# A gated-attention and mixing kernel: three stores behind a branch, and two chunks' z in one buffer

## The chip, the cores and the metric

The kernel runs on one core of a Trainium2 chip. The metric is device time in microseconds (us), the median of several executions of the same program. PE is the matrix engine, DVE the vector engine, ACT the scalar engine, POOL the general-purpose engine, and SP the engine that only issues transfers here. Each engine has its own instruction stream, executes it in order, and waits on semaphores that others count up.

## The reference

B=4, H=8, S=768, D=48. First a gated linear attention, then a token mixing of its output x (768 x 384 per batch) and a channel mixing:

```python
for t in range(S):
    state = f[:, :, t, :, None] * state + np.einsum('bhd,bhe->bhde', k[:, :, t], v[:, :, t])
    y[:, :, t] = np.einsum('bhd,bhde->bhe', q[:, :, t], state)
...
theta = x @ w_theta
zr, zi = x * np.cos(theta), x * np.sin(theta)
y = np.einsum('ts,bsd->btd', w_tok_r, zr) + np.einsum('ts,bsd->btd', w_tok_i, zi)
u = x + y
return u + np.maximum(u @ w_ch, 0.0)
```

## The kernel before

The sequence is cut into chunks of 128 tokens, six per batch, 24 in all. For every chunk the attention is computed in steps: gates (`gc`, `go`, `gs`, `ge`, `gq`, `gk`), scores, state, output (`ou`), copies of the output (`xc`, `xs`), then angles (`th`), their folding (`tn`, `se`, `ab`), sine and cosine (`tr`) and z = (x cos, x sin) (`ro`, line 434). The token mixing works on groups: two groups of 384 output tokens per batch, eight in all, and three slices of 128 channels in each; step `f` multiplies one chunk's z into one slice (L457, `pm`). After its last `f` a slice is added to x (`v`, L461), split in two float32r parts (`uh` on ACT, `ul` on DVE), run through the channel mixing (`c`, L475), finished with the maximum (`cv`, L489, DVE) and stored (`so`, L493, an SP transfer of 192 KB).

The weights are 64-bit words in memory. Sixteen parts of them are loaded (`lw`, tile `raw`, L171) and decoded in four steps: `d1` on DVE (L184), `d2` on ACT (L189), `d3` on DVE (L194, L195). Parts 2 to 13 are the token weights, 14 and 15 the channel weights `w_ch`. The raw parts and the z share one pool tag, `z`, of six buffers that are handed out in turn: the seventh tile asked for takes the buffer of the first, and its first writer waits until that one's last reader is done. In the first batch z is half as large as such a buffer, and each of its six chunks takes one.

The order on PE, ACT, DVE and POOL is written out by hand in the string table `ORDER`. SP is placed by the scheduler and executes its transfers in the order that it was given; a transfer that waits for a buffer holds up all behind it.

At the end stands a general path for inputs whose gates decay too far: a flag, computed by step `fl`, is read into a register on every engine (L575, TENSOR_LOAD), and each engine branches on it (L618). With these inputs the flag is zero and the path is skipped. On the skipping side every engine executes one EVENT_SEMAPHORE (SP eight, one for each semaphore of its transfers): it waits until all that the engine has issued is done and steps the count up by what the general path would have added, so that later waits are the same on both ways. A jump follows to the block behind the path (L690), in which SP waits for the transfers' semaphores and all engines meet twice before the program ends.

Of the kernel before, what the change touches and what calls it, by code (L numbers as in the profile page):

```python
# [8 lines left out]
F32 = mybir.dt.float32  # L9
# [8 lines left out]
B, H, S, D = 4, 8, 768, 48  # L18
DM = H * D
P = 128  # L20
NP = H // 2
C = 128
NC = S // C
HC = NC // 2
KD = DM // P
TH = 384
NTH = S // TH
# [56 lines left out]
)  # L84


# [1 line left out]
def gla_moe_kernel(  # L88
# [13 lines left out]
    nc = tc.nc  # L102

    const = ctx.enter_context(tc.tile_pool(name="const", bufs=1))
    sb = ctx.enter_context(tc.tile_pool(name="sb", bufs=1))
# [173 lines left out]
    def bank(shape, name):  # L279
        return ps.tile(shape, F32, tag="a", bufs=4, name=name)  # L280
# [95 lines left out]
    uts, xhs, xls, pths, ws, zs = ({} for _ in range(6))  # L376

    def u_tile(g):
        return sb.tile([P, KD, TH], F32, tag="ut", bufs=3, name=f"ut{g}")

    def u_slice(m):
        return uts[m // 3][:, :, m % 3 * C:(m % 3 + 1) * C]
# [6 lines left out]
    def split_xh(m, src):  # L389
        xhs[m] = sb.tile([P, KD, P], F32R, tag="xh", bufs=1, name=f"xh{m}")  # L390
        copy(nc.scalar, xhs[m], src)

    def split_xl(m, src):
        xls[m] = sb.tile([P, KD, P], F32R, tag="xl", bufs=1, name=f"xl{m}")
        nc.vector.tensor_tensor(xls[m], src, xhs[m], op=ALU.subtract)


    def angles(m, full):
        pths[m] = bank([P, DM], f"pth{m}")
        ms = ([(u_slice(m)[:, d, :], values[d // 2][:, d % 2, :]) for d in range(KD)] if full else  # L400
              [(l[:, d, :], r[:, d, :]) for l, r in ((xhs[m], wth[1]), (xhs[m], wth[0]), (xls[m], wth[1]))
               for d in range(KD)])
        for n, (l, r) in enumerate(ms):
            nc.tensor.matmul(pths[m], l, r, start=(n == 0), stop=(n == len(ms) - 1))  # L404
# [25 lines left out]
    def rotate(m, full):  # L430
        w = ws[m]
        if full:
            zs[m] = sb.tile([P, 2, DM], F32, tag="z", bufs=6, name=f"z{m}")
        nc.vector.tensor_tensor(zs[m] if full else w, w, xs[m].unsqueeze(1).to_broadcast([P, 2, DM]), op=ALU.mult)  # L434

    def split_zh(m):
        zs[m] = sb.tile([P, 2, 2, DM], F32R, tag="z", bufs=6, name=f"z{m}")
        copy(nc.scalar, zs[m][:, 1], ws[m])

    def split_zl(m):  # L440
        nc.vector.tensor_tensor(zs[m][:, 0], ws[m], zs[m][:, 1], op=ALU.subtract)
# [4 lines left out]
    def products(g, s, d, z, full):  # L446
        n, dsl = NTOK + g % NTH * NC + s, slice(d * P, (d + 1) * P)
        if s == 0:
            pms[g, d] = ps.tile([P, TH], F32, tag="mix", bufs=4, name=f"pm{g}{d}")

        if full:
            ms = [(z[:, i, dsl], values[n][:, 1 - i, :]) for i in range(2)]
        else:
            w = parts[n][2]
            ms = [(z[:, a, i, dsl], w[o][:, 1 - i, :]) for i in range(2) for a, o in ((1, 1), (1, 0), (0, 1))]
        for i, (l, r) in enumerate(ms):
            nc.tensor.matmul(pms[g, d], l, r, start=(s == 0 and i == 0), stop=(s == NC - 1 and i == len(ms) - 1))  # L457
# [33 lines left out]
    def store(b, g, d):  # L491
        th = g % NTH
        nc.sync.dma_start(out[b, d * P:(d + 1) * P, th * TH:(th + 1) * TH], uts[g][:, d, :])  # L493


    flag = const.tile([P, 1], I32, tag="flag", name="flag")
# [45 lines left out]
    def group(fn):  # L542
        return lambda n: fn(n // KD, n % KD)
# [5 lines left out]
    fn = {"h" + s: lambda n, go=go: go(n // 2, n % 2) for s, go in by_halves.items()}  # L549
# [12 lines left out]
        "f": piece, "v": group(add_u), "uh": group(split_uh), "ul": group(split_ul), "c": channels, "cv": group(finish),  # L562
        "so": group(lambda g, d: store(g // NTH, g, d)), "fl": find_worst,
    }
    done, engines = {}, {"": None, "A": nc.scalar, "D": nc.vector, "P": nc.gpsimd}
    for step in " ".join(ORDER).split():
        step, _, e = step.partition("/")
        m = done[step] = done.get(step, -1) + 1
# [3 lines left out]
    order.__exit__(None, None, None)  # L572


    rv = nc.values_load(flag[0:1, 0:1], min_val=0, max_val=P)  # L575

    def recurrence(b):
        pick = sb.tile([P, 2 * P], F32, tag="p", bufs=1, name="pick")
        nc.vector.memset(pick, 0.0)
        nc.vector.memset(pick[0:32, 47:48], 1.0)  # L580
        nc.vector.memset(pick[32:48, 47:48], 1.0)
        nc.vector.memset(pick[64:96, 111:112], 1.0)
        nc.vector.memset(pick[96:112, 111:112], 1.0)
        for p in range(NP):
            ld = []
            for nm, src in (("f", f), ("k", k), ("q", q)):
                t = sb.tile([P, NC, C], F32, tag="ut", bufs=3, name=f"r{nm}{p}")
                nc.sync.dma_start(t, src[b, :, :, p, :].rearrange("c r t -> r c t"))
                ld.append(t.rearrange("r c t -> r (c t)"))
            fr, kr, qr = ld  # L590
            zr = [sb.tile([P, 2, S], F32, tag="z", bufs=6, name=f"rz{p}{n}") for n in range(3)]
            vr, st, yt = zr[0][:, 0, :], zr[1][:, 0, :], zr[2][:, 0, :]
            kvs = [zr[0][:, 1, :], zr[1][:, 1, :]]
            nc.sync.dma_start(vr, vt[b, p])
            nc.scalar.activation(fr, fr, AF.Sigmoid)
            acc = [ps.tile([P, TH], F32, tag="mix", bufs=4, name=f"acc{p}{h}") for h in range(NTH)]
            for e in range(D):

                sel = sb.tile([P, 2, 64], F32, tag="w", bufs=2, name=f"sel{p}{e}")
                for j in range(2):  # L600
                    nc.vector.tensor_copy(sel[:, j, :], ident[:, 64 * j + e:64 * j + e + 1].to_broadcast([P, 64]))
                kv = kvs[e % 2]
                for h in range(NTH):
                    hs = slice(h * TH, (h + 1) * TH)
                    bc = bank([P, TH], f"bc{p}{e}{h}")
                    nc.tensor.matmul(bc, sel.rearrange("p j m -> p (j m)"), vr[:, hs], start=True, stop=True)
                    nc.vector.tensor_tensor(kv[:, hs], kr[:, hs], bc, op=ALU.mult)
                nc.vector.tensor_tensor_scan(st, fr, kv, 0.0, ALU.mult, ALU.add)
                nc.vector.tensor_tensor(kv, qr, st, op=ALU.mult)
                for h in range(NTH):  # L610
                    nc.tensor.matmul(acc[h], pick[:, 47 - e:47 - e + P], kv[:, h * TH:(h + 1) * TH],
                                     start=(e == 0), stop=(e == D - 1))
            for h in range(NTH):
                nc.scalar.copy(yt[:, h * TH:(h + 1) * TH], acc[h])
            for j in range(2):
                nc.sync.dma_start(xt_d[b, (2 * p + j) * D:(2 * p + j + 1) * D, :], yt[64 * j:64 * j + D, :])

    with tc.If(rv > 0, preferred_fallthrough_block=False):  # L618
        with tc.For_i(0, B, 1) as b:
            recurrence(b)  # L620
            for m in range(NC):
                if m % 3 == 0:
                    uts[m // 3] = u_tile(f"r{m}")
                nc.sync.dma_start(u_slice(m), xt_d[b, :, m * C:(m + 1) * C].rearrange("(k p) t -> p k t", p=P))
                px = bank([P, DM], f"rpx{m}")
                for d in range(KD):
                    nc.tensor.transpose(px[:, d * P:(d + 1) * P], u_slice(m)[:, d, :], ident)
                xs[m] = sb.tile([P, DM], F32, tag="x", bufs=3, name=f"rx{m}")
                nc.scalar.copy(xs[m], px)
                split_xh(m, u_slice(m))  # L630
                split_xl(m, u_slice(m))
                angles(m, False)
                for step in (whole, settle, fold, trig):
                    step(m)
                rotate(m, False)
                split_zh(m)
                split_zl(m)
            for g in range(NTH):
                for s in range(NC):
                    for d in range(KD):  # L640
                        products(g, s, d, zs[s], False)
                for d in range(KD):
                    add_u(g, d)
                    split_uh(g, d)
                    split_ul(g, d)
                for d in range(KD):
                    channel(g, d)
                    finish(g, d)
                    store(b, g, d)


def layout(inputs):
# [41 lines left out]
```

## Time and profile before

| | us |
|---|---|
| median of 3 runs | 378.42 (378.27 to 379.1) |
| the profiled execution, whole | 377.01 |
| its span, first to last instruction | 375.2 |
| PE busy / DVE busy / ACT busy | 343.1 / 278.7 / 194.0 |

The profiled execution is 1.41 us shorter than the median; 1.8 us of it lie outside the span. PE is busy for 91% of the span, but in two places it is not what the end waits for: around 56 to 85 us, where the weights are decoded, and in the last 9 us, where no engine computes.

### The profile page before, as it was taken

How to read it: one execution, taken by the hardware profiler on the slowest of the kernel's cores; microseconds unless marked ns; L12 is line 12 of the kernel's file. 1: busy time of each engine (PE TensorE's matmuls, PEld its weight loads, DVE VectorE, ACT ScalarE, POOL GpSimd, SP SyncE). 2: the span in 40 equal slices, each digit the busy share in tenths (PEclk: the TensorE clock that was granted, in tenths of full speed). 3: DMA queues.
4: the chain of work that ended last, by engine and by line, in shares of the span. 5: the costliest groups of instructions: out<-in, count | busy, mean ns of one | idle time of the engine just before them, and what ended most of it. 6: DMA issues, size and time to landing. Idle time of an engine off the chain costs nothing.

```text
span 375.2 us, 9844 instructions
## 1 busy us (share of the span) xinstructions
PE 343.1 (91%) x4176; PEld 297.0 (79%) x4176; DVE 278.7 (74%) x481; ACT 194.0 (52%) x328; POOL 56.4 (15%) x65
## 2 busy tenths in 40 slices
PE   0497797989999999999999999999999999999990
PEld 0376565656678768999999999989999999999990
DVE  5798999899898999899799589897748459132220
ACT  6498784666464787586880476846521025010100
POOL 4513330005122441110100302021000000000000
PEclk9999898999999999999999999999999999999997
DMA  7979846631244242114312455142001100011002
GB/s 267 351 266 341 269 149 224 209 117 37 83 152 135 94 116 70 49 36 140 117 45 70 156 138 153 47 123 62 0 31 35 65 2 2 0 44 54 30 3 71
DMA packets 21971, 40.82 MB, mean 109 GB/s; under 512 B 2720, under 2 KB 8864, under 8 KB 21920
## 3 DMA queue, kind: packets, MB, share of 16 engines
q1 hardware_dynamic: 21920, 40.12, 33.3%
q8 instruction: 35, 0.57, 0.6%
q14 instruction: 16, 0.13, 0.1%
HBM read 35.39 MB, written 4.72 MB: 107 GB/s over the span
## 4 chain that ended last, share of the span: by engine, by line
PE 69%; DVE 17%; DMA 6%; issue 3%; SPq 2%; ACT 1%; DVEq 0%; ACTq 0%
PE pm L457 37%; PE pch L475 9%; PE pth L404 7%; PE py L360 5%; DMA raw<-in_w_i_dram 4%; PE py L353 3%; DVE f L248 3%; PE pkv L323 2%; PE pss L294 2%; DVE value L195 2%; DVE raw L194 2%; PE psk L311 2%; DVE k L268 2%; PE pxt L373 1%; DMA f<-in_f_dram 1%
## 5 line engine op out<-in xcount | busy, mean ns | idle before, releaser
L457 PE MATMUL pm<-wp,z 128*128 128x384 f32 x648 | 124.0, 341 | 0.0
L457 PEld LDWEIGHTS pm<-wp,z 128*128 128x128 f32 x648 | 111.8, 188 | 1.6
L457 PE MATMUL pm<-value,z 128*128 128x384 f32 x144 | 52.5, 503 | 2.9 <-DVE z L434 2.9
L475 PE MATMUL pch<-uhl,wch 128*128 128x384 f32 x216 | 41.6, 340 | 0.0
L457 PEld LDWEIGHTS pm<-value,z 128*128 128x128 f32 x144 | 25.8, 191 | 18.2 <-DVE z L434 3.7
L475 PEld LDWEIGHTS pch<-uhl,wch 128*128 128x128 f32 x216 | 37.2, 188 | 0.3
L489 DVE SCALAR_TENSOR_TENSOR ut<-pch,ut 128x384 f32<-128x384 f32 x24 | 13.2, 554 | 24.9 <-PE pch L475 24.7
L263 POOL TENSOR_TENSOR q<-q,p 128x512 f32<-128x512 f32 x16 | 24.3, 1518 | 44.9 <-DMA q<-in_q_dram 20.3
L145 ACT CAST uhl<-ut 128x384 fp32r<-128x384 f32 x15 | 7.4, 509 | 44.4 <-DVE ut L461 44.4
L248 DVE TENSOR_TENSOR_SCAN f<-carry,f 128x512 f32<-128x512 f32 x24 | 29.8, 1257 | 0.0
L360 PE MATMUL py<-v,sc 128*64 128x48 f32 x768 | 28.4, 229 | 0.0
L294 PE MATMUL pss<-q,k 48*64 48x64 f32 x640 | 16.3, 237 | 12.4 <-DVE k L268 10.6
L360 PEld LDWEIGHTS py<-v,sc 128*64 128x64 f32 x768 | 25.3, 142 | 1.4
L294 PEld LDWEIGHTS pss<-q,k 48*64 48x64 f32 x640 | 13.1, 146 | 15.4 <-DVE k L268 10.6
L145 ACT COPY ut<-pxt 128x384 f32<-128x384 f32 x18 | 8.6, 477 | 29.2 <-PE pxt L373 18.2
L409 ACT ACTIVATE w<-pth 128x384 f32<-128x384 f32 x22 | 10.7, 488 | 24.3 <-PE pth L404 24.3
L461 DVE TENSOR_TENSOR ut<-pm,ut 128x384 f32<-128x384 f32 x24 | 13.1, 552 | 13.7 <-PE pm L457 13.6
L259 POOL COPY pes<-p 128x4 f32<-128x4 f32 x24 | 11.0, 458 | 81.5 <-ACT p L255 81.4
L404 PE MATMUL pth<-wth,xh 128*128 128x384 f32 x108 | 22.6, 344 | 0.0
L323 PEld LDWEIGHTS pkv<-v,ktok 64*64 64x64 f32 x640 | 12.5, 142 | 11.9 <-issue 7.4
L434 DVE TENSOR_TENSOR w<-w,x 128x768 f32<-128x768 f32 x18 | 19.5, 1086 | 2.7 <-ACT w L428 2.7
L323 PE MATMUL pkv<-v,ktok 64*64 64x48 f32 x640 | 15.0, 230 | 6.2 <-issue 4.2
(86 smaller groups left out, 595.5 us busy)
## 6 DMA issues: line engine op xcount, KB each, us to landing
f<-in_f_dram SPq DMA_DIRECT2D x24, 256.0 KB, 3.2
k<-in_k_dram SPq DMA_DIRECT2D x24, 256.0 KB, 3.2
q<-in_q_dram SPq DMA_DIRECT2D x24, 256.0 KB, 3.2
raw<-in_w_r_dram SPq DMA_DIRECT2D x12, 384.0 KB, 5.1
raw<-in_w_i_dram SPq DMA_DIRECT2D x12, 384.0 KB, 5.6
out_dram<-ut SPq DMA_DIRECT2D x24, 192.0 KB, 1.9
v<-in_v_dram SPq DMA_DIRECT2D x40, 96.0 KB, 3.1
raw<-in_w_theta_dram SPq DMA_DIRECT2D x3, 384.0 KB, 5.7
```

Of the source, the lines that this page charges most:

```text
L145: (nc.scalar.copy if on(usual) is nc.scalar else on(usual).tensor_copy)(dst, src)
L248: nc.vector.tensor_tensor_scan(fl, carry[:, pairs(h)].rearrange("p n t -> p (n t)"), fl, 0.0, ALU.mult, ALU.add)
L263: on(nc.vector).tensor_tensor(qt, qt, ps_[m][:, pairs(h)], op=ALU.mult)
L294: nc.tensor.matmul(pss[m][j][ts, p, :64], kt[r, p, ts], qt[r, p, ts], start=True, stop=True)
L323: nc.tensor.matmul(pkvs[m][t][r, p, :], kts[m][ts, p, r], vs[m][ts, t, h * D:(h + 1) * D], start=True, stop=True)
L360: nc.tensor.matmul(pys[m][j][ts, p, :], sc[j][:, p, ts if whole_chunk(m) else slice(0, 64)], vs[m][:, 0 if whole_chunk(m) else t, h * D:(h ...
L404: nc.tensor.matmul(pths[m], l, r, start=(n == 0), stop=(n == len(ms) - 1))
L434: nc.vector.tensor_tensor(zs[m] if full else w, w, xs[m].unsqueeze(1).to_broadcast([P, 2, DM]), op=ALU.mult)
L457: nc.tensor.matmul(pms[g, d], l, r, start=(s == 0 and i == 0), stop=(s == NC - 1 and i == len(ms) - 1))
L461: nc.vector.tensor_tensor(u, pms[g, d], u, op=ALU.add)
L475: nc.tensor.matmul(pcs[g, d], l, r, start=(es[0] == 0 and n == 0), stop=(es[-1] == KD - 1 and n == len(ms) - 1))
L489: nc.vector.scalar_tensor_tensor(u, pcs[g, d], 0.0, u, op0=ALU.max, op1=ALU.add)
```

## The change

Two things are changed. First, the table's end: step `rv`, the reading of the flag on every engine, now stands before the last group's channel mixing, the last three `so` are gone from the table, and the three stores are issued behind the branch. A block between the general path and the program's end holds them. There SP waits for DVE's count as it is behind the branch. Because the skipping side steps this count up in one instruction, after DVE's last work, none of the three values exists before that.

Second, in the first batch the z of chunks 0 and 1, 2 and 3, 4 and 5 share a buffer, so that three z tiles are handed out instead of six. The general path is rearranged too, since it may no longer use the buffer that the waiting stores read from; it is not executed with these inputs.

```diff
-    "f f v uh f ul f f f f f v uh f ul f f f f c v uh c ul c cv cv so cv so so",
+    "f f v uh f ul f f f f f v uh f ul f f f f rv c v uh c ul c cv cv cv",
...
         if full:
-            zs[m] = sb.tile([P, 2, DM], F32, tag="z", bufs=6, name=f"z{m}")
+
+            if m % 2 == 0:
+                two = sb.tile([P, 2, 2, DM], F32, tag="z", bufs=6, name=f"z{m}")
+                zs[m], zs[m + 1] = two[:, 0], two[:, 1]
...
+    over = []
+
+    def load_flag(_):
+        over.append(nc.values_load(flag[0:1, 0:1], min_val=0, max_val=P))
+
+    fn["rv"] = load_flag
...
-    rv = nc.values_load(flag[0:1, 0:1], min_val=0, max_val=P)
+
+    LAST = B * NTH - 1
...
-    with tc.If(rv > 0, preferred_fallthrough_block=False):
+    with tc.If(over[0] > 0, preferred_fallthrough_block=False):
...
                     store(b, g, d)
+    for d in range(KD):
+        store(B - 1, LAST, d)
```

DVE at the program's end, before (`uhl` is the float32r split, `ut` the group's u, `pch` the channel mixing in PSUM; line numbers of the kernel before):

```order
L461 TENSOR_TENSOR ut_3855<-pm_4340,ut_3855 128x384
L468 TENSOR_TENSOR uhl_4394<-ut_3855,uhl_4394 128x384
L489 SCALAR_TENSOR_TENSOR ut_3855<-pch_4381,ut_3855 128x384
L489 SCALAR_TENSOR_TENSOR ut_3855<-pch_4385,ut_3855 128x384
L489 SCALAR_TENSOR_TENSOR ut_3855<-pch_4389,ut_3855 128x384
L575 TENSOR_LOAD flag
L618 COMPARE_AND_BRANCH
L618 UNCONDITIONAL_BRANCH
```

And now (lines of the changed kernel):

```order
L571 TENSOR_LOAD flag
L464 TENSOR_TENSOR ut_3852<-pm_4337,ut_3852 128x384
L471 TENSOR_TENSOR uhl_4405<-ut_3852,uhl_4405 128x384
L492 SCALAR_TENSOR_TENSOR ut_3852<-pch_4392,ut_3852 128x384
L492 SCALAR_TENSOR_TENSOR ut_3852<-pch_4396,ut_3852 128x384
L492 SCALAR_TENSOR_TENSOR ut_3852<-pch_4400,ut_3852 128x384
L623 COMPARE_AND_BRANCH
L623 UNCONDITIONAL_BRANCH
```

The reading of the flag has moved from behind the last three finishes to before the last addition; on PE it has moved likewise, from behind the last 27 matmuls to before them. On SP it stays where it was, long before the end.

SP's loads in the middle of the first batch, before (`raw` with `w_r`, `w_i`: token weights, parts 12 and 13; `w_ch`: parts 14 and 15):

```order
L514 DMA k_768<-in_k_dram 128x512
L525 DMA v_86<-in_v_dram 64x384
L514 DMA q_844<-in_q_dram 128x512
L171 DMA raw_820<-in_w_r_dram 128x768
L171 DMA raw_820<-in_w_i_dram 128x768
L525 DMA v_85<-in_v_dram 64x384 x2
L171 DMA raw_850<-in_w_r_dram 128x768
L171 DMA raw_850<-in_w_i_dram 128x768
L514 DMA k_869<-in_k_dram 128x512
L171 DMA raw_883<-in_w_ch_dram 128x768 x2
L514 DMA q_929<-in_q_dram 128x512
L525 DMA v_86<-in_v_dram 64x384
```

And now:

```order
L517 DMA k_767<-in_k_dram 128x512
L171 DMA raw_819<-in_w_r_dram 128x768
L171 DMA raw_819<-in_w_i_dram 128x768
L517 DMA q_843<-in_q_dram 128x512
L528 DMA v_85<-in_v_dram 64x384 x2
L171 DMA raw_849<-in_w_r_dram 128x768
L171 DMA raw_849<-in_w_i_dram 128x768
L517 DMA k_868<-in_k_dram 128x512
L171 DMA raw_882<-in_w_ch_dram 128x768 x2
L528 DMA v_86<-in_v_dram 64x384
L171 DMA raw_940<-in_w_ch_dram 128x768
L517 DMA q_928<-in_q_dram 128x512
```

Part 12 (`raw_820`, now `raw_819`) has moved ahead of a q load, and one v load of chunk 7 behind the channel weights. Part 12 now takes the buffer of part 7, which DVE reads last in its L195, where before it took that of part 8, read last by the L195 that stands two decodes later. On PE, ACT, DVE and POOL the order of the work is the same but for the reading of the flag, and no wait of one of these engines on another is added.

## Rows read from the trace of the kernel before

**Rows 1.** The page's first line.
```profile
span 375.2 us, 9844 instructions
```
**Rows 2.** Chain that ended last, from 340 us: start, us, what.
```profile
366.15 0.56 DVE ut L489
```
**Rows 3.** Timeline of SP, 360 to 376 us: start, us, engine, line, operation.
```profile
365.74 1.34 SPq L493 DMA_DIRECT2D out_dram<-ut  x3
```
**Rows 4.** Instructions of tile flag: durations ns min/median/max, first and last start us.
```profile
L575 PEldq TENSOR_LOAD <-flag x1: 487/487/487, 363.3 to 363.3; - x1
L575 DVEq TENSOR_LOAD <-flag x1: 795/795/795, 366.2 to 366.2; - x1
```
**Rows 5.** Instructions of line 618, the branch and its skipping side; columns likewise.
```profile
L618 SPq EVENT_SEMAPHORE  x8: 17/17/17, 370.2 to 371.0; - x8
...
L618 PEldq COMPARE_BRANCH  x2: 95/1994/3893, 363.9 to 366.3; - x2
L618 SPq COMPARE_BRANCH  x2: 38/46/53, 367.1 to 371.1; - x2
L618 DVEq COMPARE_BRANCH  x2: 51/53/55, 367.4 to 367.6; - x2
...
L618 DVEq EVENT_SEMAPHORE  x1: 21/21/21, 367.5 to 367.5; - x1
```
**Rows 6.** Instructions of line 690, the program's end; columns likewise.
```profile
L690 SPq EVENT_SEMAPHORE  x10: 17/28/28, 373.9 to 375.1; - x10
...
L690 SPq DRAIN  x3: 7/7/13, 374.4 to 374.7; - x3
...
L690 PEldq DRAIN  x2: 8/40/73, 370.3 to 374.8; - x2
L690 DVEq DRAIN  x2: 10/36/63, 371.2 to 374.7; - x2
```
**Rows 7.** Transfers issued 366.7 to 367.0 us: the third store, KB, us to landing.
```profile
out_dram<-ut SPq DMA_DIRECT2D x1, 192.0 KB, 3.8
```
**Rows 8.** Transfers issued 365.7 to 365.9 us: the first store.
```profile
out_dram<-ut SPq DMA_DIRECT2D x1, 192.0 KB, 1.9
```
**Rows 9.** DMA queues, 366 to 376 us: packets, MB, share of 16 engines.
```profile
q8 instruction: 2, 0.03, 1.4%
```
**Rows 10.** Waits of SP, 340 to 376 us: us in total, times, longest.
```profile
SPq L493 <- DVE ut L489: 26.6, 4, 17.9
```
**Rows 11.** Timeline of DVE, 340 to 376 us; in brackets idle before, and what ended it.
```profile
361.47 0.56 DVE L461 TENSOR_TENSOR ut<-pm,ut 128x384 f32<-128x384 f32 x1 [4.49 <-PE pm L457]
```
**Rows 12.** Timeline of ACT, 56 to 72 us.
```profile
68.15 0.94 ACT L189 ACTIVATE raw<-raw 128x768 f32<-128x768 f32 x1 [4.41 <-DMA raw<-in_w_i_dram]
69.00 0.45 ACT L145 COPY ut<-pxt 128x384 f32<-128x384 f32 x1
```
**Rows 13.** Timeline of DVE, 56 to 100 us.
```profile
55.60 1.25 DVE L195 SCALAR_TENSOR_TENSOR value<-raw 128x768 int32<-128x768 int32 x1
...
68.14 0.56 DVE L184 TENSOR_SCALAR raw<-raw 128x768 int32<-128x768 int32 x1
69.87 0.55 DVE L415 SCALAR_TENSOR_TENSOR w<-w,pth 128x384 f32<-128x384 f32 x1 [1.16 <-ACT w L409]
```
**Rows 14.** Timeline of PE, 40 to 135 us.
```profile
67.82 0.49 PE L373 MATMUL pxt<-ident,x 128*128 128x128 f32 x3
...
84.40 6.72 PE L457 MATMUL pm<-value,z 128*128 128x384 f32 x20 [0.98 <-DVE z L434]
```
**Rows 15.** Timeline of SP, 53 to 63 us.
```profile
56.58 0.48 SPq L525 DMA_DIRECT2D v<-in_v_dram  x1
...
62.92 0.42 SPq L171 DMA_DIRECT2D raw<-in_w_i_dram  x1
```
**Rows 16.** Instructions of line 684, the program's first block.
```profile
L684 SPq EVENT_SEMAPHORE  x1: 17/17/17, 0.7 to 0.7; - x1
```
**Rows 17.** Timeline from 0 to 1.3 us.
```profile
0.82 0.87 SPq L514 DMA_DIRECT2D f<-in_f_dram  x2
```

More of the change, by code (lines that the diff above doesn't have):

```diff
@@ L584, in recurrence @@
         for p in range(NP):
[L585 to L593, printed above, removed]
+            zr = [sb.tile([P, 2, S], F32, tag="z", bufs=6, name=f"rz{p}{n}") for n in range(4)]
+            fr, kr, qr, vr, st, yt, *kvs = [t[:, i, :] for t in zr for i in range(2)]
+            for t, src in ((fr, f), (kr, k), (qr, q)):
+                nc.sync.dma_start(t.rearrange("r (c t) -> r c t", c=NC), src[b, :, :, p, :].rearrange("c r t -> r c t"))
             nc.sync.dma_start(vr, vt[b, p])
@@ L621, in gla_moe_kernel @@
             for m in range(NC):
-                if m % 3 == 0:
-                    uts[m // 3] = u_tile(f"r{m}")
+                if m == 0:
+                    uts[0] = u_tile("r")
+                uts[1] = uts[LAST]
                 nc.sync.dma_start(u_slice(m), xt_d[b, :, m * C:(m + 1) * C].rearrange("(k p) t -> p k t", p=P))
```

## The prediction

> **What bounds the kernel now.** I read the end first, since the change is there. The chain of waits ends with the last finish on DVE, which follows PE's last matmul and runs from 366.15 to 366.71 us [rows 2]; the span ends at 375.2 [rows 1]. So 8.5 us pass after the last computation. SP's rows split them: the third store is issued in the last third of 1.34 us from 365.74, at 366.75, and ends at 367.08 [rows 3]. SP branches at 367.1 and stands in its first EVENT_SEMAPHORE until 370.2; eight of them take until 371.0; it jumps at 371.1 [rows 5] and has its first instruction behind the jump at 373.9 [rows 6]. From there to the end are 1.3 us. PE and DVE pay for such a jump too, PE from 366.3 to 370.3, DVE from 367.6 to 371.2 [rows 5, 6], but in the shadow of SP. The end is thus: issue, landing, 0.8 of waits, 2.8 of jump, 1.3 of meeting, all in a row on SP.
>
> For the second part I looked at 56 to 85 us. ACT sits idle 4.41 us for the load of weight part 12, whose second half is issued at 62.92, up to 68.15 [rows 12, 15]. Behind it in ACT's order are a copy of x (69.00) and the step that DVE waits 1.16 us for at 69.87 [rows 12, 13]. DVE is then busy almost without a gap up to the z that PE waits 0.98 us for at 84.40 [rows 14].
>
> **The branch taken early.** SP's last store ahead of the branch belongs to the group before, and then SP stands 17.9 us waiting for DVE [rows 10]. Its eight waits and its jump, 0.8 and 2.8 us [rows 5, 6], now fall into that time: 3.6 us leave the path. If that cover were gone they would come back whole.
>
> **What it costs: the stores are later.** The first store waits for a count that DVE reaches only by its EVENT_SEMAPHORE behind the branch, so not at 365.74, when its own finish is done, but after the last of the three finishes. DVE's last finish ends at 366.71 [rows 2]. Before, the EVENT_SEMAPHORE came at 367.5, with a TENSOR_LOAD of 795 ns from 366.2 and the branch ahead of it [rows 4, 5]; that load is now done earlier. I take 366.8 for it, 367.5 as the upper bound. An issue takes about 0.33 and three of them, one behind the other, some 0.38 apart (an estimate from the 1.34 us of rows 3, which also hold waits for DVE), so the third goes out at 366.85 + 0.76 = 367.6 instead of 366.75: 0.85 later, at most 1.55.
>
> What this makes of the landing has two bounds. The third store lands 3.8 us after its issue [rows 7], the first 1.9 [rows 8]. Between them fetches of instructions, 0.03 MB in one of two queues, run on the same transfer engines [rows 9], released by the jumps of PE and DVE. If the delay belongs to these fetches and not to the store, the landing hardly moves: undisturbed it would be 367.6 + 1.9 = 369.5. If the 3.8 go with the store it is 371.4. From the second of SP's final waits, at about 373.95, to the end are 1.25 us [rows 1, 6], so the span would end at 370.75 to 372.65. But PE and DVE have to arrive as well: PE at 370.3 as now, DVE at 366.9 + 3.6 = 370.5 [rows 5, 6], and from SP's first DRAIN to the end are 0.8 us, which gives no less than 371.3. Between 371.3 and 372.65 I take 372.2, nearer to the third store's row, since three stores now stand behind the fetches where two did. Gain: 375.2 - 372.2 = **3.0 us** (2.55 to 3.9; 1.8 with DVE's upper bound).
>
> **The flag read earlier.** On PE the load of 487 ns began at 363.3 while its matmuls ran to 366.15 [rows 2, 4]: PE's sequencer was 2.8 us ahead of its array and the load did not stop it. Ahead of the last 27 matmuls it stands behind a long run of matmuls without waits, so the same lead covers it; uncovered it costs 0.5 to 0.6. DVE's 0.8 stand in the 4.49 us that it waits before the last addition [rows 11]; ACT waits as long. I take nothing.
>
> [...] The jumps that left a gap (PE 4.0, DVE 3.6, SP 2.8) all go over the general path. From the program's first block to the next, which lies right behind it, SP goes from 0.7 to 0.82 [rows 16, 17]. The new block with the stores lies right ahead of the program's end, so I count one gap for each engine and not two. [...]
>
> **The shared z.** Part 12 now takes part 7's buffer, which DVE's L195 leaves at 55.60 + 1.25 = 56.85 [rows 13]; SP has just got there, at 56.58 [rows 15]. So its second half is issued near 57.3 instead of 62.92 and, with the 5.2 us that it took (62.92 to ACT's start at 68.15) or some more, lands by 64, while ACT is free and idle. ACT's next task, the copy, then waits for PE's transposes, 67.82 + 0.49 = 68.31 [rows 14], instead of starting at 69.00 [rows 12]: 0.69 us earlier. DVE is done with part 12's first step at 68.70 [rows 13], in time. So DVE's step comes at about 69.2 instead of 69.87, all that follows without a gap moves with it, and PE's 0.98 us at 84.40 can take the whole of it. I take **0.65 us** (0, if some other chain is as long, to 0.98). Part 13 is not earlier: SP still waits for PE's last read of the old v ahead of it. The channel weights come earlier, and nothing waited for them. The v load that goes behind them is for chunk 7, in the second batch, whose products stand on PE behind all the angles of the first.
>
> **The sum.** Against the profiled execution: 377.01 - 3.0 - 0.65 = 373.4, a span of 371.55. The median of the runs shown is 1.41 above that execution, and I subtract the same 3.65 from it: 378.42 - 3.65 = **374.8 us**.
>
> **Rivals.** (1) Two gaps: the new block costs PE and DVE a second jump. PE would reach the end at 370.3 + 4.0 = 374.3, and with 0.8 the span ends at 375.1: the tail gains 0.1, the second part stays, 377.7. Against it speaks that SP passes from block to block in 0.1 us [rows 16, 17]. (2) The early load gains nothing, or slows part 11, which is still in flight when part 12 starts; both ACT and DVE stand in its wait. Any delay under 0.65 is taken back at the wait of 69.87, so this one ends near 378.42 - 3.0 = 375.4. [...] (3) Slower than before: a second jump, with three engines fetching at once where two did. Its place is the join, its price one more jump h on PE; the span ends at 370.3 + h + 0.8, less 0.65, and is longer than before by over 0.2% from h = 5.5 on. SP alone took 2.8, two together 4.0; by the same step three would take 5.2, at worst 6.0 (an estimate), which gives 377.01 + 1.25 and a median of 379.7. It needs what rival 1 needs and contention besides.
>
> **How the numbers follow.** The forecast, 70%: 373.5 to 375.6, from tail 2.55 to 3.9 and second part 0.3 to 0.98. Rival 2, 14%: 374.5 to 376.4. Rival 1, 11%: 377.7, just at the bound. Rival 3, 3%: 379.7. The other 2% is a gain beyond both bounds. The range 373.4 to 376.7 holds the forecast, rival 2 and the late DVE count, and leaves out the other rivals and some noise. A measurement can tell about 0.2%, 0.76 us, from no change: faster holds the forecast, rival 2, the 2% and half of rival 1, 91%; same 6%; slower 3%.
>
> **What the profile after would show.** Right: SP's eight waits of the branch before 355 us; the three stores in a row from about 366.85, none at 365.7; no gap of 2.8 us on SP at the end; PE's and DVE's DRAIN near 370.5 less 0.65; no idle gap in PE at the last 27 matmuls; ACT's wait of 4.41 us ended by PE's transposes, and PE's 0.98 us shrunk to 0.3. Wrong: a second gap on PE or DVE between stores and end, a third store landing much more than 4 us after its issue, or PE idle ahead of its last 27 matmuls.

## The result

The changed kernel takes **373.75 us** (median of 12 runs, 371.21 to 377.55), the kernel before 378.11 us beside it (median of 12 runs, 374.76 to 379.69). The ratio is 0.989, 95% interval 0.9854 to 0.9926: of 378.11 us that is 4.2 us gained, 2.8 to 5.5. Forecast were 374.8 us and a gain of 3.65; the time lies in the range, 373.4 to 376.7. The profiled execution of the changed kernel took 373.69 us, 3.32 less than that of before, which lay 1.1 below its median; each trace is one execution. Ratios leave out runs that were slow as a whole, and the one trace of such a run, that of the shared z alone, is read in its stage only.

**The end.** The rows that answer to [rows 1 to 9]: the page's first line, the last computations of the chain, the branch (now line 623) and the program's end (now line 698). Columns are those of the groups of before.

```profile
span 372.0 us, 9844 instructions
```
```profile
345.90 14.58 PE pm L460 x84
360.49 4.70 PE pch L478 x27
365.18 0.02 issue
365.21 0.56 DVE ut L492
```
```profile
L623 SPq EVENT_SEMAPHORE  x8: 17/17/17, 347.0 to 348.5; - x8
...
L623 SPq COMPARE_BRANCH  x2: 38/46/53, 346.9 to 348.5; - x2
...
L623 DVEq COMPARE_BRANCH  x2: 51/53/55, 365.2 to 366.3; - x2
...
L623 DVEq EVENT_SEMAPHORE  x1: 21/21/21, 365.8 to 365.8; - x1
```
```profile
L698 SPq EVENT_SEMAPHORE  x10: 17/28/28, 370.3 to 371.9; - x10
...
L698 SPq DRAIN  x3: 7/7/13, 371.2 to 371.5; - x3
...
L698 PEldq DRAIN  x2: 8/40/73, 369.0 to 371.5; - x2
L698 DVEq DRAIN  x2: 10/34/58, 370.5 to 371.5; - x2
```

SP's timeline, and the third store's transfer (KB, us to landing):

```profile
365.90 1.89 SPq L496 DMA_DIRECT2D out_dram<-ut  x3
```
```profile
out_dram<-ut SPq DMA_DIRECT2D x2, 192.0 KB, 4.0
```

SP's waits stand at 347 to 348.5 us and its jump right behind them, in the shadow of PE, and no second gap stands at the end. The last finish ends at 365.21 + 0.56 = 365.76 (before: 366.71), and the stores start 0.13 later. They take 1.89 us, since the third issue alone takes 1.03. The third store, issued at 366.75, has landed at 370.70. From the last finish to the end, which I call the **tail**, there are 371.98 - 365.76 = 6.22 us, and before 375.21 - 366.71 = 8.49 [rows 1, 2]: 2.27 gained. The other 0.95 us were gained ahead of the last finish.

**The shared z.** ACT, DVE and PE at the places of [rows 12 to 14], and SP's issue of the second half of part 12 [rows 15], each from its own timeline:

```profile
64.51 0.93 ACT L189 ACTIVATE raw<-raw 128x768 f32<-128x768 f32 x1 [0.41 <-DMA raw<-in_w_i_dram]
68.70 0.48 ACT L145 COPY ut<-pxt 128x384 f32<-128x384 f32 x1 [3.27 <-PE pxt L373]
```
```profile
69.61 0.56 DVE L415 SCALAR_TENSOR_TENSOR w<-w,pth 128x384 f32<-128x384 f32 x1 [0.74 <-ACT w L409]
```
```profile
84.16 6.72 PE L460 MATMUL pm<-value,z 128*128 128x384 f32 x20 [0.38 <-DVE z L437]
```
```profile
58.02 0.42 SPq L171 DMA_DIRECT2D raw<-in_w_i_dram  x1
```

The long wait of ACT is now one for PE's transposes. Set against the end of these, DVE's step at 69.61 comes 0.94 us later and came 1.56 later before: 0.62 earlier. PE's wait at z has gone from 0.98 to 0.38 us.

Part 12 came early by its place on SP as well as by its buffer. In the kernel before it stood behind a q load that SP held until PE's L353 was done, at 62.0 us; now it stands ahead of that load. SP's longest wait from 56 us on, before and now:

```profile
SPq L514 <- PE py L353: 5.0, 1, 5.0
```
```profile
SPq L517 <- PE py L353: 4.0, 1, 4.0
```

### The profile page after: what moved, and what is told of

Read it like the earlier page. It is cut to its first block, busy times and chain, and to the rows that moved or that the text cites. A ratio compares the mean times of both kernels' runs of the same rounds, so it can differ in the third digit from the quotient of the medians.

```text
span 372.0 us, 9844 instructions
## 1 busy us (share of the span) xinstructions
PE 344.0 (92%) x4176; PEld 297.8 (80%) x4176; DVE 273.3 (73%) x481; ACT 193.8 (52%) x328; POOL 57.1 (15%) x65
## 2 busy tenths in 40 slices
DMA packets 21971, 40.82 MB, mean 110 GB/s; under 512 B 2720, under 2 KB 8864, under 8 KB 21920
## 4 chain that ended last, share of the span: by engine, by line
PE 85%; DVE 6%; DMA 3%; issue 2%; SPq 1%; ACT 1%; DVEq 0%
PE pm L460 43%; PE pch L478 10%; PE pth L404 9%; PE py L360 6%; PE py L353 4%; PE pkv L323 3%; PE pss L294 3%; PE psk L311 3%; DMA raw<-in_w_i_dram 2%; PE pxt L373 2%; DVE value L195 1%; DMA f<-in_f_dram 1%; PE pss L289 1%; DVE raw L194 1%; DVE f L248 1%
## 5 line engine op out<-in xcount | busy, mean ns | idle before, releaser
L460 PE MATMUL pm<-value,z 128*128 128x384 f32 x144 | 54.0, 514 | 1.7 <-DVE z L437 1.7
L263 POOL TENSOR_TENSOR q<-q,p 128x512 f32<-128x512 f32 x16 | 26.2, 1640 | 45.7 <-DMA q<-in_q_dram 34.5
L248 DVE TENSOR_TENSOR_SCAN f<-carry,f 128x512 f32<-128x512 f32 x24 | 28.7, 1214 | 0.0
L259 POOL COPY pes<-p 128x4 f32<-128x4 f32 x24 | 9.5, 398 | 81.4 <-ACT p L255 81.4
L437 DVE TENSOR_TENSOR w<-w,x 128x768 f32<-128x768 f32 x18 | 18.4, 1024 | 3.8 <-ACT w L428 3.8
L238 POOL TENSOR_SCALAR f<-f 128x512 f32<-128x512 f32 x8 | 13.6, 1699 | 48.5 <-DMA f<-in_f_dram 38.3
```

The costliest lines, as they stand in the source:

```text
L238: on(nc.vector).tensor_scalar(ft, ft, F_MIN, None, op0=ALU.max)
L248: nc.vector.tensor_tensor_scan(fl, carry[:, pairs(h)].rearrange("p n t -> p (n t)"), fl, 0.0, ALU.mult, ALU.add)
L263: on(nc.vector).tensor_tensor(qt, qt, ps_[m][:, pairs(h)], op=ALU.mult)
```

## The experiments

### The end alone

The changed kernel with the z of before:

```diff
-            if m % 2 == 0:
-                two = sb.tile([P, 2, 2, DM], F32, tag="z", bufs=6, name=f"z{m}")
-                zs[m], zs[m + 1] = two[:, 0], two[:, 1]
+            zs[m] = sb.tile([P, 2, DM], F32, tag="z", bufs=6, name=f"z{m}")
```

> Only the first part: the flag read early, the three stores behind the branch, but each chunk's z of the first batch in a buffer of its own as before. Theory (two separate gains): the stretch from the end of DVE's last finish to the end of the span, 8.5 us before, is 6.2 us as with both parts; part 12 comes late as before, ACT waits about 4.4 us for it and PE about 1.0 us for the z of chunk 4. Time 2.3 us below the kernel before. Rival (the shared z gives nothing, and what the changed kernel gained ahead of the end was chance): the same stretch at the end, and a time as low as with both parts, 3.5 to 4.4 us below the kernel before.

Measured: 373.67 us, ratio 0.9898 (0.9863 to 0.9934): 3.8 us below the kernel before, 2.5 to 5.2. That is more than the 2.3 of the theory and in the span of the rival, and the two kernels' ratios, 0.9898 here and 0.989 with both parts, can't be told apart; so what the shared z is worth is read from its stage and not from the whole time. The tail is 5.36 us, 3.13 less than before and 0.8 less than expected. SP and DVE at the end of this kernel (SP's timeline; its end, line 695):

```profile
366.01 2.37 SPq L493 DMA_DIRECT2D out_dram<-ut  x3
```
```profile
L695 SPq DRAIN  x3: 7/7/13, 370.4 to 370.7; - x3
...
L695 DVEq DRAIN  x2: 10/36/61, 369.3 to 370.8; - x2
```

Here the second issue takes 1.50 us, so the third store goes out 2.07 us after the last finish. It is the later one of the two kernels, yet it lands earlier, 4.09 after the last finish against 4.94. In the run with only the last pair in one buffer it is the same (issued 2.10, landed 4.25 us after the last finish). So here a third store that goes out when the fetches of instructions are nearly through lands earlier than one that goes among them. At 68 us all is as before: ACT waits 4.23 us for part 12 and PE 0.79 for z.

### The shared z alone

```diff
-            zs[m] = sb.tile([P, 2, DM], F32, tag="z", bufs=6, name=f"z{m}")
+            if m % 2 == 0:
+                two = sb.tile([P, 2, 2, DM], F32, tag="z", bufs=6, name=f"z{m}")
+                zs[m], zs[m + 1] = two[:, 0], two[:, 1]
```

> Only the second part: pairs of chunks of the first batch share a buffer for z; stores and flag as before. Theory: from the start of chunk 1's z on DVE to PE's run of 20 matmuls on chunk 4's z it takes 26.3 us instead of 26.9, since part 12 lands before ACT has other work; 8.5 us from the last finish to the end as before; time 0.6 us below the kernel before, which is little more than the scatter. Rival: the whole 0.95 us and more by which the last finish came earlier belong to the shared z, then 1.0 to 1.9 us below. Other rival: nothing is gained, the stretch takes 26.9.

Measured: 376.16 us, ratio 0.9961 (0.9932 to 0.9991): 1.5 us, 0.3 to 2.6, which holds the 0.6 of the theory and the 1.0 to 1.9 of the rival. In the trace (span 378.08 us) the stretch that I expected at 26.3 us took 28.95, with a granted clock of 0.50 from 58 to 62 us, and the tail was 7.86 instead of 8.5, so neither was met. At the stage itself it is as with both parts: DVE's step comes 0.94 us after the transposes, and PE waits 0.37 for z:

```profile
86.75 5.43 PE L460 MATMUL pm<-value,z 128*128 128x384 f32 x16 [0.37 <-DVE z L437]
```

### No general path at all

The kernel before without the flag's load, the branch and the path; no engine jumps.

> The kernel before without the branch and the general path (left out: the path for gates that decay too far, which these inputs do not take), so that no engine jumps and no instruction is fetched at the end. Theory (the third store lands 3.8 us after its issue because a transfer engine is busy with fetches that the jumps cause): it lands about 1.9 us after its issue, and from the last finish to the end it takes 0.04 + 1.9 + 1.25 = 3.2 us instead of 8.5; time 5.3 us below the kernel before. Rival (the 3.8 belong to three stores in a row): landing still 3.5 to 3.9, 5.0 to 5.2 us to the end, time 3.4 us below.

Measured: 372.96 us, ratio 0.9891 (0.9852 to 0.993): 4.1 us, 2.6 to 5.6, which doesn't decide between 5.3 and the rival's 3.4. The tail is 4.14 us, between the two as well, so the branch cost 8.49 - 4.14 = 4.35 of the old tail, and the change takes 2.3 to 3.1 of that. The third store's transfer (KB, us to landing):

```profile
out_dram<-ut SPq DMA_DIRECT2D x1, 192.0 KB, 3.1
```

A transfer counts its semaphore up sixteen times (2720 counts for 170 transfers, in the trace of before as in that of the changed kernel). I take each count for one part of it, and the last one for its landing. Fifteen of the third store's parts land by 1.92 us after its issue, the last one at 3.10, with a single fetch of 8 KB in that stretch. The first two stores, with no fetch beside them, have all sixteen in after 1.87 and 1.94 us.

### The flag alone read early

```diff
-    "... c v uh c ul c cv cv so cv so so",
+    "... rv c v uh c ul c cv cv so cv so so",
```

> Only the early reading of the flag; the three stores stay ahead of the branch, z as before. Theory: the load of 0.5 us on PE and 0.8 us on DVE hide, PE has no gap ahead of its last 27 matmuls, DVE's EVENT_SEMAPHORE of the branch comes 0.04 us after the end of its last finish instead of 0.8, but SP's chain does not hold it: 8.5 us from the last finish to the end, as before, within 0.3. Rival (the load stops PE): 0.5 to 0.6 us of idle time ahead of the last 27 matmuls.

Measured: 376.98 us (a single time). SP's rows of the branch:

```profile
L623 SPq EVENT_SEMAPHORE  x8: 17/17/17, 369.7 to 371.1; - x8
...
L623 SPq COMPARE_BRANCH  x2: 37/45/53, 367.0 to 371.2; - x2
```

They stand where they stood before [rows 5], and the tail is 8.69 us. DVE steps its count 0.04 us after its last finish. Reading the flag early costs nothing here, and by itself it gains nothing: SP still waits for its stores and then jumps.

### Two of the stores ahead of the branch

```diff
-    "... c ul c cv cv cv",
+    "... c ul c cv cv so cv so",
...
-    for d in range(KD):
-        store(B - 1, LAST, d)
+    store(B - 1, LAST, KD - 1)
```

> The changed kernel, but only the third of the last stores is given behind the branch; the first two stand ahead of it, as before, and the flag is read early. Theory (what the branch costs is covered only while SP has no transfer of the last group in flight ahead of it): SP's eight waits stand at the end again until the second store has landed, about 3 us after the last finish, then the jump of 2.8 us, so that the third store is issued 6 to 7 us after the last finish and the span ends about 10 us after it, 1 to 2 us more than the kernel before (8.49) and 3 to 4 more than the changed kernel (6.22). Rival (moving the reading of the flag and the last store is enough, SP's jump is covered by PE's and DVE's jumps anyhow): the tail is 6.2 or less.

Measured: 376.76 us (a single time), and a tail of 10.86 us, longer than before by 2.4. SP's rows of the branch, then its third store:

```profile
L623 SPq EVENT_SEMAPHORE  x8: 17/17/17, 368.3 to 368.8; - x8
...
L623 SPq COMPARE_BRANCH  x2: 38/46/53, 364.1 to 368.9; - x2
```
```profile
371.64 0.34 SPq L496 DMA_DIRECT2D out_dram<-ut  x1
```

SP waits at the branch until the second store has landed, whose last part comes 4.6 us after its issue, at 368.3, while the other fifteen were there by 365.6; that is why the third store is later than expected. SP jumps from 368.9 to 371.5, and only then issues the third. That store, beside a single fetch of 8 KB, lands in 2.1 us. The price of a lost cover is the one that the prediction named, the jump and the waits in a row.

### One store instead of three

The changed kernel, with the last group stored in one transfer of 576 KB:

```diff
-    for d in range(KD):
-        store(B - 1, LAST, d)
+    nc.sync.dma_start(out[B - 1, :, (NTH - 1) * TH:].rearrange("(d p) t -> p d t", p=P), uts[LAST])
```

> The changed kernel, but the last group's three stores of 192 KB are one transfer of 576 KB behind the branch. In the changed kernel the three were issued 0.13, 0.52 and 0.99 us after the last finish, the third issue took 1.03 us, and the third store landed 4.94 us after the last finish; last finish to end of span was 6.22 us. Theory (part of the landing goes with the position in the row of issues, part with the fetches that stand beside it): the one issue starts 0.13 after the last finish, all 576 KB have landed 2.1 to 4.1 us after it, and from the last finish to the end it is 5.2 to 5.5 us, 0.7 to 1.0 less than the changed kernel; it is then the best of all, at a ratio of about 0.985 to 0.989 against the kernel before. Rival (the landing is set by the instruction fetches alone, which end at the same time whatever SP issues): landing at 4.5 to 5 and a tail of 6.0 to 6.3, no gain against the changed kernel. Second rival (one transfer of three slices is cut into the same parts, and issuing it takes three times as long): issue about 1 us, no gain either.

Measured: 373.02 us, ratio 0.9879 (0.9829 to 0.993), not to be told from the changed kernel's 0.989. The issue is early and short (0.14 after the last finish, 0.39 long), yet the transfer lands after 5.1 us, and the tail is 6.49. My theory expected 5.2 to 5.5; the first rival is right that there is no gain, though the landing and the tail are later than its 4.5 to 5 and 6.0 to 6.3 too. Its DMA from 365.4 to 371.4 us, in slices of 0.15 us, with the two queues of instruction fetches (packets, MB, share of 16 engines) and the transfer, then the program's end:

```profile
GB/s 0 0 0 0 0 0 324 338 328 317 403 348 317 389 317 348 266 62 51 51 51 51 51 41 75 0 130 0 0 0 0 0 0 0 0 0 0 0 0 0
...
q8 instruction: 2, 0.03, 1.8%
q14 instruction: 2, 0.02, 0.6%
...
out_dram<-ut SPq DMA_DIRECT2D x1, 576.0 KB, 5.1
```
```profile
L697 SPq DRAIN  x3: 7/7/13, 370.6 to 371.3; - x3
...
L697 DVEq DRAIN  x2: 10/34/58, 370.9 to 371.3; - x2
```

The bulk runs at some 340 GB/s and is through by 368.1; then come 0.9 us at 50. By the counts on the transfer's semaphore, 14 of the 16 parts land 2.8 to 3.0 us after the issue, the other two after 4.2 and 5.1. DVE, which jumps too, is here later than SP (370.9 against 370.6): its jump took 5.1 us from 365.8, against 3.6 in the kernel before [rows 5, 6].

### One store, and nothing fetched by jumps

The same transfer after the last finish in the kernel without a general path:

```diff
-    "... f f f f c v uh c ul c cv cv so cv so so",
+    "... f f f f c v uh c ul c cv cv cv so",
```

> The same without the general path, and the last group's three stores as one transfer of 576 KB after the last finish; to be set beside the run with the one transfer behind the branch, where 14 of its 16 parts landed 2.8 to 3.0 us after the issue and the other two 4.2 and 5.1. Theory (the two late parts share their transfer engines with the fetches, and the others don't): all 16 parts land 2.5 to 3.1 us after the issue, with at most one later by some single fetch, and the tail is 3.9 to 4.5 us. Rival (576 KB in one piece is uneven over the 16 engines by itself): two parts are late by 1 us or more here too, and the tail is 5.5 or more.

Measured: 376.23 us (a single time). The last finish ended at 369.85, 3 us later than before, and only what follows it is read. DMA from 369.9 us on, in the same slices:

```profile
GB/s 0 0 0 0 0 0 205 444 348 328 369 358 369 348 399 369 277 72 20 31 20 31 0 0 0 0 0 0 0 0 0 0 0 0 0 0 0 0 0 0
```
```profile
q14 instruction: 1, 0.01, 0.9%
...
out_dram<-ut SPq DMA_DIRECT2D x1, 576.0 KB, 3.8
```

Fifteen of 16 parts land 2.8 to 3.0 us after the issue, as the 14 of the run before, and a single one, beside a single fetch, at 3.8. The tail is 4.68 us, 0.2 more than expected. So the bulk of this store takes the same time with and without jumps; what is late in the stretches with fetches is one part or two, and the end waits for all sixteen.

### Three stores in a row, and nothing fetched by jumps

Meant to issue all three after the last finish in the kernel without a general path, the last slice first:

```diff
-        "so": group(lambda g, d: store(g // NTH, g, d)),
+        "so": group(lambda g, d: store(g // NTH, g, KD - 1 - d if g == B * NTH - 1 else d)),
```

> The kernel before without the general path, its flag and its branch (as in the run without the path), but the last group's three stores are given in the reverse order, the one whose finish comes last first, so that all three go out one behind the other after the last finish, as in the changed kernel, and no engine jumps. The general path isn't there, which these inputs don't use. Theory (the changed kernel's landing, 3.95 us from the third issue, is made by the instruction fetches that the jumps of PE and DVE set off): issues at about +0.05, +0.4 and +0.8 us after the last finish, each taking 0.33; the third store lands 1.9 to 2.3 us after its issue, at +2.6 to +3.2 after the last finish, and the tail is 3.6 to 4.3 us, about that of the run without the path (4.14). Rival (three transfers that go out in one row delay one another): the third lands 3.5 to 4 us after its issue and the tail is 5.5 to 6.2 as in the changed kernel.

The order on SP came out as before, at 0.98 and 0.50 us ahead of the last finish and 0.03 behind it, so nothing was tested of what was expected, and whether three stores in a row delay one another stays untested. What it shows is the run without the path once more: 370.02 us (a single time), third store landed 2.35 us after its issue, tail 3.38. So even without jumps the tail is 3.4 to 4.1, by when one part comes.

### Only the last pair of chunks in one buffer

```diff
-            if m % 2 == 0:
+            if m < 4:
+                zs[m] = sb.tile([P, 2, DM], F32, tag="z", bufs=6, name=f"z{m}")
+            elif m == 4:
```

> The changed kernel's end as it is, but of the first batch's z only those of chunks 4 and 5 share a buffer, so that weight part 12 takes the buffer of part 8 as in the kernel before and SP's loads of parts 12 and 13 stand where they did. Theory (the gain of the shared z is that part 12 takes an earlier buffer): as without sharing: ACT waits 4.2 to 4.9 us for part 12, whose d2 starts at 66.5 to 68.4; DVE's settle of chunk 3 ends 1.4 to 2.0 us after the transposes of chunk 4; PE waits 0.8 to 1.5 us at the z of chunk 4. Rival (the gain comes from fewer z tiles in hand, or from an earlier load of the channel weights): 0.94 us from transposes to settle and 0.4 us of PE's wait, as with all three pairs shared.

Measured: 373.87 us (a single time). ACT and PE at the two places:

```profile
68.03 0.95 ACT L189 ACTIVATE raw<-raw 128x768 f32<-128x768 f32 x1 [3.92 <-DMA raw<-in_w_i_dram]
```
```profile
84.31 6.72 PE L461 MATMUL pm<-value,z 128*128 128x384 f32 x20 [0.52 <-DVE z L438]
```

Part 12 is as late as without sharing, as the theory said (ACT's wait of 3.92 is a little under the 4.2 that I gave). But DVE's step comes only 1.08 us after the transposes, and PE waits 0.52: less than I expected (1.4 to 2.0, and 0.8 to 1.5), and by these two figures alone the rival is as near. Against it speaks that ACT's copy still follows part 12 without idle time, at 68.88, where in the changed kernel it waits 3.27 us for the transposes. The transposes themselves ended late, at 68.68 us, after a stretch at a lower clock than before (busy time of PE, PE's weight loads, DVE, ACT and POOL from 58 to 62 us, then the granted clock, the DMA share and GB/s):

```profile
58.00:62.00 4.00, 3.95 (x38) 2.18 (x38) 3.93 (x7) 1.91 (x4) 0.00 (x0) 0.50 0.46 162
```

The granted clock is 0.50 here; before, the same stretch shows 0.63. So what the shared z gains is the time by which part 12 comes later than the transposes let ACT go on, and that goes with the clock: over the seven kernels with part 12 late, DVE's step lies behind the transposes by 1.08 us at a granted clock of 0.50 in this stretch, by 1.56 at 0.63, by 1.39 at 0.68, and by 1.91 to 2.58 in the four at 1.00. In the four with the three shared pairs it is 0.94 at any of these. At before's clock the shared z gains 0.62, in this run it would have gained 0.14, and at 1.00 it would gain some 1.0 or more (estimates from these differences).

The end of this kernel is that of the changed one, and its tail is 5.52 us, with a second issue of 1.54 us as in the run of the end alone.

## Why the prediction was right, step by step

**The branch taken early: right.** 3.6 us of waits and jump have left the path. Two runs undo the cover in two ways (flag early with all stores ahead, two stores ahead), and both times SP's waits and jump are back at the end.

**The stores' delay: right.** I had the first at 0.1 to 0.15 us after the last finish and the third at 0.9; they are at 0.13 and 0.99.

**The landing: the term that was mis-sized.** I put the third landing at 2.8 to 4.7 us after the last finish (369.5 to 371.4 against 366.71); it was 4.94, outside. From that landing to the end it is 1.28 us, as I took it (1.25). In the profile the tail gains 2.27 instead of 3.0, below my lower bound of 2.55. The same end gained 3.13 and 2.97 in the two kernels that share it, so 3.0 was not wrong for this end, but my bounds were too narrow: they took a store's landing and an issue of 0.33 us as fixed. The runs show in their place that in stretches with fetches one or two parts of a store land 0.3 to 2.7 us behind the others, and that one of SP's three issues takes 1.0 or 1.5 us instead of 0.33. In all three kernels with this end a fetch of 16 KB runs during that long issue; but it is also an issue that follows the one before it at once, and as the run that was to send out three stores in a row without jumps did not do so, the two causes aren't separated. DVE's jump, which I took at 3.6 us, varies too, from its branch to its DRAIN: 3.2 and 3.4 us in the two kernels with the short tail, 4.2 in the changed one, 5.1 with one large store. A delay of the fetch by the store would do that, but with the flag alone read early it is 4.4 beside stores as before, so this isn't settled. That the late parts share their transfer engines with the fetches fits their number in the two runs with one large store (two with fetches of two queues, one with one), but the trace doesn't name the engine, and this is inferred. Why DVE's jump starts 0.14 us after the last finish in some runs (those with the short tail among them) and 0.50 in others is open, and with it which of the two tails comes.

**The flag: right.** In the chain of the changed kernel the last 27 matmuls follow the 84 before them without a gap, and DVE's wait is 4.49 us as before [rows 11]:

```profile
360.52 0.56 DVE L464 TENSOR_TENSOR ut<-pm,ut 128x384 f32<-128x384 f32 x1 [4.49 <-PE pm L460]
```

**The second jump: right.** SP's jump at 348.5 lies in its wait for DVE, its stores follow DVE's count at 365.80 by 0.1 us, and PE's DRAIN comes 3.23 us after the last finish against 3.55 before. Rivals 1 and 3 fall with it. PE, DVE and SP have one stall each (3.6, 4.2 and 2.5 us) and none where the new block passes into the program's end: with one store SP's first instruction there stands at 365.9 us, 0.1 behind the issue. ACT and POOL, which branch over the same path, reach the end's block 0.39 and 0.12 us after their branch; neither the sum nor a rival asked why, and no run shows it.

**The shared z: right, and its size goes with the clock.** 0.65 forecast; 0.62 at DVE's step and 0.60 at PE's wait. In all eleven traces z comes 14.46 to 14.50 us after that step, so whatever the step gains arrives. But 0.62 is its size at the clock of these two executions; by the seven traces it would be anything from 0.14 to 1.0 and more, which I had not seen, so that the forecast came so near is in part luck. Part 12 took 6.5 us from its issue at 58.02 to ACT's start, not 5.2, and was still early: ACT then stood idle 3.27 us. Part 11 was not slowed, its second half landed 3.7 us after its issue and before the change 4.8. Rival 2 falls by this stage; the whole times could not have told it from the forecast. Its upper bound of 376.4 follows from no term of the sum (the late DVE count gives 376.6, a tail gain of 2.55 gives 375.9).

**What the sum left out.** Ahead of the last finish 0.95 us were gained, and at most 0.62 of them belong to the shared z: the transposes ended 0.36 us later than before, so PE's run on z began only 0.24 earlier. The rest lies behind 84 us, where the two programs are alike: from PE's run on z to the last finish it is 282.31 us before and 281.61 after. This is not the change's. It varies by over 2 us between kernels that are equal there, and the next rows show what it goes with. POOL's and DVE's timelines, from the kernel before:

```profile
123.49 1.49 POOL L263 TENSOR_TENSOR q<-q,p 128x512 f32<-128x512 f32 x1 [4.51 <-DMA q<-in_q_dram]
123.77 2.29 DVE L248 TENSOR_TENSOR_SCAN f<-carry,f 128x512 f32<-128x512 f32 x1
```

and from the changed one:

```profile
123.94 1.22 DVE L248 TENSOR_TENSOR_SCAN f<-carry,f 128x512 f32<-128x512 f32 x1
124.10 2.12 POOL L263 TENSOR_TENSOR q<-q,p 128x512 f32<-128x512 f32 x1 [5.67 <-DMA q<-in_q_dram]
```

Where POOL starts first, DVE's operation ends 1.08 us after POOL's, which is its own length of 1.2 less 0.12, as if it had stood still until then. Where DVE starts first, it takes 1.22, and POOL 2.12 instead of some 1.3. At 261 us the same happens to z (1.93 us on DVE behind POOL's 261.52 to 262.81 before, 0.95 in the changed kernel, where POOL's 2.08 come second). In these four places the one that starts second takes 0.8 to 1.1 us more than its own length (1.2, 0.95 and 1.3); by what it is held up, no run shows. I added up by how much DVE's operations behind 85 us exceed the shortest of their kind, where by over a quarter. Leaving out the trace of the shared z alone: in five traces that sum is 3.0 to 4.0 us, and the stretch from z to the last finish takes 281.3 to 282.1; in the other five it is 4.7 to 7.6, and the stretch takes 282.3 to 283.7. Within the five the order is not kept (the largest sum, 7.6, stands with 282.3, and 6.4 with 283.7), and that the one causes the other was not tried.

So that the profiled gain, 3.32 us, came near the forecast of 3.65 is partly luck: the tail gave 0.7 less than I took, and 0.3 that is not the change's stands in its place. Nor could the median have told so little: its interval is 1.4 us to either side, where I had counted on 0.76.

## What to carry to other kernels

Where an engine arrives at a branch with work still in flight, the waits and the jump can stand in a row at the end (0.8 and 2.8 us on SP here); move the reading of the condition and the branch ahead of the last wait on that engine, and issue what is left behind the branch, all of it: with two of the three stores left ahead the tail was 10.86 us instead of 6.22. What is then issued beside other engines' jumps, while their instructions are fetched, can land late (here 14 parts of 16 by 3.0 us and the last at 5.1), so bound its landing by the slowest of sixteen parts and not by the bulk. Of a load that is moved forward, count only up to the next thing that the same engine waits for, and ask on what that depends.

## What the runs showed of the hardware that I had not expected

- SP's issue of a store of 192 KB took 0.33 us ahead of the branch. Of the issues behind it one took 1.03 us (changed kernel), one 1.50 (the end alone) and one 1.54 (the last pair in one buffer), where instructions of other engines are fetched and the issues follow each other at once; which of the two does it is open.
- The sixteen parts of a store of 192 KB with no fetch beside it landed by 1.87 and 1.94 us after the issue (no general path). In stretches with fetches one or two came later: 14 after 2.8 to 3.0 us, two after 4.2 and 5.1 (one store of 576 KB). That these meet a fetch on their transfer engine is inferred.
- DVE's scan that started during POOL's product of two tiles ended its own length less 0.12 us after it (2.29 us instead of 1.2, kernel before at 123.77); the other way round POOL took 2.12 instead of 1.3 (changed kernel at 124.10).
- In 58 to 62 us the granted clock was anything from 0.50 to 1.00 on average, in executions of almost the same program, behind an idle time of PE of 1.3 to 1.9 us. The length of that idle time doesn't order them: 1.80 us stands ahead of 1.00, and 1.83 ahead of 0.50.
